# A fused attention and MLP block: layernorm's eps as a fifth triple of statistics, and another order of the first tiles' statistics and applies

## The chip, the core and the metric

The kernel runs on one core of a Trainium2 chip. A core has five engines that work side by side and tell each other by semaphores when something is done: TensorE (PE: matrix multiplications and transposes by a unit matrix; its weight loads are shown as PEld), VectorE (DVE), ScalarE (ACT), GpSimd (POOL) and SyncE (SP, which here only issues transfers). Each engine takes its instructions in the order in which the program lists them. The metric is the time of one execution on the device in microseconds (us), the median of several.

## The reference

```python
x = A_x                                   # 1 x 2048 x 640, bf16
xn = _layernorm(x, axis=-1)               # (x - mean) / sqrt(var + 1e-5)
return x + _A_ref(xn, A_wqkv, A_w_phi, A_wo) + _B_ref(xn, B_w1, B_w3, B_w2)

# _A_ref: linear attention, 32 heads of 20
q, k, v = ...                             # (xn @ wqkv), cut into heads
pq, pk = q @ w_phi, k @ w_phi             # per head, 20 x 20
phi_q = concatenate([softmax(pq), softmax(-pq)])
phi_k = concatenate([softmax(pk), softmax(-pk)])
kv, z = phi_k^T @ v, sum of phi_k over the tokens
o = (phi_q @ kv) / (phi_q @ z + 1e-6)
return o @ wo

# _B_ref: gated MLP, inner width 1536
return (silu(xn @ w1) * (xn @ w3)) @ w2
```

## The kernel before, in words

The 2048 tokens are cut into 16 tiles of 128, which lie on the 128 partitions. Each tile of x (x_tok) is normalized in place and then transposed into xnT, where the model dimension of 640 lies on the partitions in five chunks of 128. For the tiles 0 to 3 the transposes run on TensorE, with copies out of PSUM by ScalarE (three copies for tile 0, of two, two and one chunks; two copies for the others; one of tile 3's by VectorE); for the tiles 4 to 15 transfers do them.

From xnT come the values (wv), the keys (Wkp: the key weights with w_phi folded in), the queries (Wqp) and the MLP. Exponentials of the keys go to ekt and are divided by their sums (reduction on VectorE, multiplication on POOL). Then TensorE sums the products of keys and values over all tiles (tiles v,ekt in the profile), the queries are projected, normalized, transposed by a transfer (eqT) and multiplied with those sums. The MLP's matmuls of 128x512 (xnT,w_s) are spread between all this. At the end each output tile adds the attention's projection (wo), the MLP's second matmul (w2) and x itself (xres).

The order is made by a planner in the kernel. Fourteen streams (norms, transposes, attention, queries, mlps and others) offer their next step; `_Program` keeps a clock for each engine from the costs given with each operation, and the step that could begin first is taken. So a change in one early step can change the order of steps much later. What a step waits for is found from the memory that its operations read and write; the order on each engine is that in which the steps were taken. Almost all instructions are recorded by the two helpers `op` (line 102) and `dma` (line 114), so the profile shows them under L102 and L114, and one goes by the tiles' names.

What touches the start:

- `first_loads` issues tile 0 in two halves on SP, tile 1 on ScalarE's queue, then tile 2 on SP, the two halves of wv (one on each of the two queues), tile 3, and the first parts of w1 and w3 on SP.
- `warm_up` gives TensorE IDLE1 small matmuls on a tile of zeros (shown as `PS<-t`) before there is anything to do; after tile 0's transposes IDLE2 more follow.
- The statistics of a tile are two `bn_stats` of 320 columns each (`ln_half`; BATCH_NORM_STATS2 in the profile). Each leaves two triples in `bst`, for every second element: a count, a mean, and the count times the variance. `bn_aggr` (BATCH_NORM_AGGREGATE) merges the four triples into mean and variance (`mv`). Then eps is added, on VectorE for the tiles 0 to 3 and on POOL for the others, and POOL raises to the power -0.5 (`rstd`).
- Tile 1's statistics are ScalarE's: a sum (`act_sum` with Copy), which VectorE scales by -1/640 to the negative mean (`scalar_op`), and a sum of squares around that mean. `act_rstd` divides by 640, adds eps and takes the power.
- `ln_apply` subtracts the mean and multiplies by rstd: on VectorE for the tiles 0 to 3, on VectorE or ScalarE for the others, whichever the planner has free sooner.

The stream `norms` sets the order of the first steps:

```python
yield lambda: act_sum(1, ACT.Copy, bst[:, 1, 0:1])
yield lambda: (ln_half(0, 0), ln_half(0, 1), ln_rstd(0, 1))
yield lambda: scalar_op(1, mv[:, 1, 0:1], bst[:, 1, 0:1], -1.0 / D, 0.0)
yield lambda: act_sum(1, ACT.Square, mv[:, 1, 1:2], mv[:, 1, 0:1])
yield lambda: ln_apply(0)
yield lambda: act_rstd(1)
yield lambda: (ln_half(2, 0), ln_half(2, 1))
yield lambda: ln_apply(1)
```

Of the kernel before, what the change touches and what calls it, by code (L numbers as in the profile page):

```python
# [3 lines left out]
ACT = mybir.ActivationFunctionType  # L4
ALU = mybir.AluOpType
# [4 lines left out]
D = 640  # L10
# [3 lines left out]
T = S // 128  # L14
# [4 lines left out]
EPS = 1e-5  # L19
# [230 lines left out]
def bass_parallel_sum__linear_kernel_hedgehog__glu_gated_swiglu__prompt_kernel(  # L250
# [11 lines left out]
    bf = DT.bfloat16  # L262
    LAG = 4.0
    QLEAD = 2
    IDLE1, IDLE2 = 45, 5
    f32 = DT.float32
    P = _Program(nc)

# [5 lines left out]
    def region(size):  # L274
        o = top[0]
        top[0] = o + (size + 31) // 32 * 32
        assert top[0] <= arena_size, top[0]
        return a0 + o

    def new(name, shape, dtype, offset=None):  # L280
        size = mybir.dt.size(dtype)
        for n in shape[1:]:
            size *= n
        return P.sbuf(name, shape, dtype, region(size) if offset is None else offset)
# [2 lines left out]
    GM = new("GM", [128, DC, H], bf)  # L287
    phi_s = new("phi_s", [128, DC, DH], bf)
    BDc = new("BDc", [128, DC, 8 * DH], bf)
    bst = new("bst", [128, T, 12], f32)  # L290
    mv = new("mv", [128, T, 2], f32)
    rstd = new("rstd", [128, T, 2], f32)
    mhalf = new("mhalf", [128, 4], f32)
# [13 lines left out]
    x_tok = new("x_tok", [128, T, D], bf, RX)  # L307
# [53 lines left out]
    def free(ap):  # L361
        n = 1
        for s in ap.shape[1:]:
            n *= s
        return n

    def act(o, i, f, scale=1.0):
        P.op("ACT", "activation", [o], [i], (o, i, f), dict(scale=scale),
             cost=0.17 + free(o) / 1200)
# [21 lines left out]
    def memset(eng, o, v):  # L391
        P.op(eng, "memset", [o], [], (o, v), cost=0.15 + free(o) / 960)

    def select(o, base, pattern, cm, cmp, fill):
        P.op("POOL", "affine_select", [o], [o], (),
             dict(out=o, in_=o, compare_op=cmp, fill=fill, base=base, pattern=pattern,
                  channel_multiplier=cm), cost=0.3 + free(o) / 960)
# [16 lines left out]
    def first_loads():  # L414
        def half_wv(eng, a):
            P.dma(eng, wv[:, :, a:a + 320], wqkv_t[:, :, 2 * D + a:2 * D + a + 320])

        P.dma("SP", x_tok[:, 0, 0:320], x_t[:, 0, 0:320])
        P.dma("ACT", x_tok[:, 1, :], x_t[:, 1, :])
        P.dma("SP", x_tok[:, 0, 320:D], x_t[:, 0, 320:D])  # L420
        load_x(2, 3)
        half_wv("ACT", 0)
        half_wv("SP", 320)
        load_x(3, 4)
        w13(0, 512)
        P.dma("SP", phi_s[:], phi_t)
        P.dma("SP", wqkT[:, DC:2 * DC, :], A_wqkv[:, D:2 * D], True)
        load_x(4, 8)
        load_x(8, 12)
        load_x(12, 16)  # L430
        P.dma("SP", wqkT[:, 0:DC, :], A_wqkv[:, 0:D], True)


    def consts():
        memset("DVE", t1[:, 2, 0:128], 0.0)
        memset("DVE", warm[:], 0.0)
        act(warm[:], warm[:], ACT.Exp)
        memset("POOL", ident[:], 0.0)
        select(ident[:], 0, [[-1, 128]], 1, ALU.not_equal, 1.0)
        memset("POOL", GM[:], 1.0)  # L440
        select(GM[:], 0, [[128, DC], [-DH, H]], 1, ALU.is_ge, 0.0)
        select(GM[:], DH, [[-128, DC], [DH, H]], -1, ALU.is_gt, 0.0)
        memset("POOL", mhalf[:], -0.5)
        memset("POOL", M3[:, 0:3], 1.0)
        select(M3[:, 0:3], 0, [[-40, 3]], 1, ALU.is_ge, 0.0)
        select(M3[:, 0:3], 40, [[40, 3]], -1, ALU.is_gt, 0.0)
        memset("POOL", ekt[:, T * 2 * D:T * 2 * D + 48], 1.0)

    def v_heads(a):
        return a.rearrange("p (g x) -> p g x", x=64)[:, :, 0:63].rearrange("p g (h c) -> p g h c", c=21)  # L450

    def ln_half(t, q):
        i, o = x_tok[:, t, 320 * q:320 * q + 320], bst[:, t, 6 * q:6 * q + 6]
        P.op("DVE", "bn_stats", [o], [i], (o, i), cost=0.48)

    def ln_rstd(t0, n):
        for t in range(t0, t0 + n):
            o, i = mv[:, t, 0:2], bst[:, t, 0:12]
            P.op("DVE", "bn_aggr", [o], [i], (o, i), cost=0.22)
        m, v, r, z = mv[:, t0:t0 + n, 0], mv[:, t0:t0 + n, 1], rstd[:, t0:t0 + n, 0], rstd[:, t0:t0 + n, 1]  # L460
        if t0 < 4:
            P.op("DVE", "tensor_scalar", [r], [v], (),
                 dict(out=r, in0=v, scalar1=EPS, scalar2=None, op0=ALU.add), cost=0.13)
        else:
            P.op("POOL", "tensor_scalar_add", [r], [v], (r, v, EPS), cost=0.25)
        P.op("POOL", "tensor_tensor", [r], [r, mhalf[:, 0:n]], (r, r, mhalf[:, 0:n], ALU.pow),
             cost=0.57 if t0 < 4 else 0.73)
        if t0 >= 4:
            P.op("POOL", "tensor_scalar_mul", [z], [m], (z, m, -1.0), cost=0.25)
            P.op("POOL", "tensor_tensor", [z], [z, r], (z, z, r, ALU.mult), cost=0.25)  # L470

    def act_sum(t, f, o, bias=None):
        j = t1[:].rearrange("p n c -> p (n c)")[:, 0:D]
        i = x_tok[:, t, :]
        kw = dict(accum_out=o)
        if bias is not None:
            kw["bias"] = bias
        P.op("ACT", "activation", [j, o], [i] + ([] if bias is None else [bias]), (j, i, f), kw, cost=0.75)

    def scalar_op(t, o, i, a, b):  # L480
        P.op("DVE", "tensor_scalar", [o], [i], (),
             dict(out=o, in0=i, scalar1=a, scalar2=b, op0=ALU.mult, op1=ALU.add), cost=0.15)

    def act_rstd(t):
        scalar_op(t, rstd[:, t, 0:1], mv[:, t, 1:2], 1.0 / D, EPS)
        r = rstd[:, t, 0:1]
        P.op("POOL", "tensor_tensor", [r], [r, mhalf[:, 0:1]], (r, r, mhalf[:, 0:1], ALU.pow), cost=0.57)

    def ln_stats(t0, n):
        for t in range(t0, t0 + n):  # L490
            ln_half(t, 0)
            ln_half(t, 1)
        ln_rstd(t0, n)

    def ln_apply(t):
        o, m, s, z = x_tok[:, t, :], mv[:, t, 0:1], rstd[:, t, 0:1], rstd[:, t, 1:2]
        if t < 4 or P.free["DVE"] < P.free["ACT"] + 0.45:
            P.op("DVE", "tensor_scalar", [o], [o, m, s],
                 (o, o, m, s, ALU.add if t == 1 else ALU.subtract, ALU.mult),
                 cost=0.4)  # L500
        else:
            P.op("ACT", "activation", [o], [o, s, z], (o, o, ACT.Identity), dict(bias=z, scale=s),
                 cost=0.9)
# [227 lines left out]

    def norms():
        yield lambda: (first_loads(), consts())
        yield lambda: act_sum(1, ACT.Copy, bst[:, 1, 0:1])
        yield lambda: (ln_half(0, 0), ln_half(0, 1), ln_rstd(0, 1))
        yield lambda: scalar_op(1, mv[:, 1, 0:1], bst[:, 1, 0:1], -1.0 / D, 0.0)
        yield lambda: act_sum(1, ACT.Square, mv[:, 1, 1:2], mv[:, 1, 0:1])
        yield lambda: ln_apply(0)
        done["ln"] = 1
        yield lambda: act_rstd(1)  # L740
        yield lambda: (ln_half(2, 0), ln_half(2, 1))
        yield lambda: ln_apply(1)
        done["ln"] = 2
        yield lambda: ln_rstd(2, 1)
        yield lambda: ln_apply(2)
        done["ln"] = 3
        yield lambda: (ln_half(3, 0), ln_half(3, 1), ln_rstd(3, 1))
        yield lambda: ln_apply(3)
        done["ln"] = 4
        while done["t"] < 4:  # L750
            yield None
        yield lambda: memset("DVE", v_heads(v2[:].rearrange("p t n -> p (t n)"))[:, :, :, DH], 1.0)
        yield block_diag
        done["bd"] = 1
        todo = []
        for t in range(4, T + 2, 2):
            if t == T or t > done["k"] + 8:
                for u in todo:
                    yield lambda u=u: ln_apply(u)
                    done["ln"] = u + 1  # L760
                todo = []
            if t == T:
                break
            while t > done["k"] + 8:
                yield None
            yield lambda t=t: ln_stats(t, 2)
            for u in todo:
                yield lambda u=u: ln_apply(u)
                done["ln"] = u + 1
            todo = [t, t + 1]  # L770
# [166 lines left out]
    n = len(streams)  # L937
    heads, alive = [None] * n, [True] * n
    while any(alive):
        best = None  # L940
        for i in range(n):
            if heads[i] is None and alive[i]:
                s = next(streams[i], StopIteration)
# [28 lines left out]
        i, ops, after = best[2:]  # L972
# [65 lines left out]
```

## Time and profile before

| what | value |
|---|---|
| median of 3 runs | 268.09 us (268.03 to 268.10) |
| profiled execution | 267.97 us |
| its span, first to last instruction | 266.2 us |
| TensorE busy | 261.4 us, 98% of the span |
| VectorE, ScalarE, POOL busy | 168.0, 101.5, 100.6 us |
| granted TensorE clock | 1.000 over the span |
| HBM read, written | 12.81 MB, 2.62 MB |

How to read the lines that follow. A line of a group gives the engine, the operation, what it writes <- what it reads, partitions x elements, how often, the busy time in us and the mean of one in ns, and behind the second bar the idle time of the engine before it and what ended it. A line of the timeline gives start in us, duration in us, engine, line, operation, tiles; several instructions in a row are drawn together with their number behind an x, and the time from the first start to the last end. In brackets stands the idle time before. A line of the chain of waits gives start, duration and what it was. A line of the waits gives who waited for whom: us in total, how many times, the longest. A line on a transfer gives the queue, the size and the time from its issue to its landing. A line on one tile's instructions gives how many, their shortest, median and longest duration in ns, and the first and last start. Matmuls are pipelined: the duration of one is longer than the distance to the next. A few records of matmuls can be missing.

### The profile page before, as it was taken

The page shows a single profiled execution, that of the slowest core. Times are in us where ns is not written, and L with a number is a line of the kernel's source. Part 1 is how long each engine was busy: PE and PEld are TensorE (multiplying, and loading weights), DVE is VectorE, ACT ScalarE, POOL GpSimd, SP SyncE. Part 2 cuts the span into 40 slices and gives each one's busy share as a digit, 9 for nine tenths or more (in the row PEclk, how much of TensorE's full clock was granted, in tenths as well). Part 3 has the DMA queues.
Part 4 walks back from the last instruction along what each step waited for, and adds up shares of the span by engine and source line. Part 5 has one row for each costly group of instructions (what it writes and reads, how often), then busy time and mean ns, then how long its engine had stood idle before and what let it go on. Part 6 is the DMA issues. An engine that isn't in the chain of part 4 may idle for free.

```text
span 266.2 us, 4851 instructions
## 1 busy us (share of the span) xinstructions
PE 261.4 (98%) x1965; PEld 162.1 (61%) x1986; DVE 168.0 (63%) x289; ACT 101.5 (38%) x201; POOL 100.6 (38%) x143
## 2 busy tenths in 40 slices
PE   8999999999999999999999999999999999999996
PEld 7665777777655555545454545544577777777773
DVE  3469998998766979798898787888511121212112
ACT  5677999887326254433432343322100000000000
POOL 4314896999984444454624243430000000000000
PEclk9999999999999999999999999999999999999999
DMA  7998793760383254444454433063212212131201
GB/s 213 300 321 164 106 263 27 177 219 0 110 276 72 57 113 89 84 81 79 79 81 79 81 77 70 14 85 74 49 52 75 76 58 90 52 98 52 87 36 49
DMA packets 63510, 27.73 MB, mean 104 GB/s; under 512 B 49920, under 2 KB 63488, under 8 KB 63488
## 3 DMA queue, kind: packets, MB, share of 16 engines
q1 hardware_dynamic: 62544, 26.82, 43.6%
q10 hardware_dynamic: 944, 0.61, 0.7%
q8 instruction: 15, 0.25, 0.4%
q14 instruction: 7, 0.06, 0.1%
HBM read 12.81 MB, written 2.62 MB: 58 GB/s over the span
## 4 chain that ended last, share of the span: by engine, by line
PE 96%; DMA 1%; DVE 1%; issue 1%; POOL 0%
PE PS L102 96%; DMA x_tok<-in_A_x_dram 1%; DVE bst L102 0%; POOL rstd L102 0%; DVE x_tok L102 0%; DVE mv L102 0%; DVE xres L102 0%; DVE rstd L102 0%
## 5 line engine op out<-in xcount | busy, mean ns | idle before, releaser
L102 PE MATMUL PS<-xnT,w_s 128*128 128x512 bf16 x463 | 105.7, 379 | 1.0 <-issue 0.2
L102 PEld LDWEIGHTS PS<-xnT,w_s 128*128 128x128 bf16 x480 | 45.5, 98 | 50.7 <-DVE xnT L102 0.3
L102 PE MATMUL PS<-w_s,hT 128*128 128x320 bf16 (+2 forms) x384 | 54.9, 299 | 0.0
L102 DVE TENSOR_TENSOR xres<-PS,xres 128x640 bf16<-128x640 f32 (+2 forms) x17 | 13.4, 786 | 59.8 <-PE PS L102 59.8
L102 ACT ACTIVATE th<-PS 128x512 f32<-128x512 f32 x48 | 29.0, 603 | 49.8 <-PE PS L102 49.8
L102 PEld LDWEIGHTS PS<-w_s,hT 128*128 128x128 bf16 x384 | 37.1, 98 | 15.1
L102 DVE SCALAR_TENSOR_TENSOR t<-th,PS 128x512 bf16<-128x512 f32 x48 | 32.6, 680 | 16.0 <-ACT th L102 15.7
L102 POOL TENSOR_TENSOR ekt<-ekt,rS 128x640 bf16<-128x640 bf16 x32 | 39.6, 1276 | 2.6 <-DVE rS L102 2.6
L102 DVE SCALAR_TENSOR_TENSOR hT<-t,PS 128x512 bf16<-128x512 bf16 x48 | 33.0, 687 | 5.7 <-DVE t L102 0.9
L102 ACT ACTIVATE eq<-PS 128x600 bf16<-128x600 f32 (+1 forms) x72 | 23.9, 418 | 29.3 <-PE PS L102 29.3
L102 PE MATMUL PS<-wv,xnT 128*128 128x320 bf16 x160 | 24.5, 299 | 0.0
L102 PE MATMUL PS<-wo_s,oT 128*128 128x320 bf16 (+2 forms) x159 | 24.3, 298 | 0.1
L102 PE MATMUL PS<-Wqp,xnT 128*128 128x512 bf16 (+1 forms) x157 | 23.7, 297 | 0.2
L102 PE MATMUL PS<-Wkp,xnT 128*128 128x320 bf16 x160 | 23.7, 299 | 0.0
L102 POOL TENSOR_TENSOR eq<-eq,rq 128x600 bf16<-128x600 bf16 (+1 forms) x32 | 22.7, 730 | 1.3
L102 POOL TENSOR_TENSOR half<-eq 128x660 f32<-128x660 bf16 x15 | 20.4, 1359 | 7.0 <-ACT eq L102 7.0
L102 DVE TENSOR_REDUCE S<-ekt 128x64 f32<-128x1280 bf16 x16 | 22.9, 1432 | 0.0
L102 POOL TENSOR_TENSOR rq<-rq,Sq 128x32 f32<-128x32 f32 x16 | 4.1, 255 | 47.7 <-DVE rq L102 35.5
L102 ACT ACTIVATE ekt<-PS 128x640 bf16<-128x640 f32 x32 | 20.9, 733 | 2.5 <-PE PS L102 2.5
L102 PEld LDWEIGHTS PS<-Wqp,xnT 128*128 128x128 bf16 x160 | 13.2, 98 | 11.6
L102 PEld LDWEIGHTS PS<-wo_s,oT 128*128 128x128 bf16 x160 | 15.5, 98 | 6.5
L102 PEld LDWEIGHTS PS<-wv,xnT 128*128 128x128 bf16 x160 | 15.3, 98 | 6.3 <-ACT xnT L102 0.4
(56 smaller groups left out, 184.0 us busy)
## 6 DMA issues: line engine op xcount, KB each, us to landing
w_s<-in_B_w_dram SPq DMA_DIRECT2D x6, 640.0 KB, 6.1
xres<-in_A_x_dram SPq DMA_DIRECT2D x16, 160.0 KB, 2.4
out_dram<-xres SPq DMA_DIRECT2D x15, 160.0 KB, 1.8
x_tok<-in_A_x_dram SPq DMA_DIRECT2D x3, 640.0 KB, 6.4
w_s<-in_B_w_dram SPq DMA_DIRECT2D x1, 1920.0 KB, 8.4
wo_s<-in_A_wo_dram SPq DMA_DIRECT2D x1, 800.0 KB, 7.2
wv<-in_A_wqkv_dram ACTq DMA_DIRECT2D x1, 400.0 KB, 4.1
wv<-in_A_wqkv_dram SPq DMA_DIRECT2D x1, 400.0 KB, 5.2
```

The source lines that it names most:

```text
L102: o = _Op(eng, lambda: m(*args, **kw), r, w, cost)
```

## The change

Five edits.

1. `bst` gets three more columns per tile, a fifth triple: count 0, mean 0, and 640 x eps. `consts` writes them with two memsets on VectorE. `bn_aggr` reads 15 numbers instead of 12, so that its variance comes out with eps added. The additions of eps in `ln_rstd` (VectorE for the tiles 0, 2 and 3, POOL for 4 to 15) go, and POOL's power reads `mv` directly.
2. Tile 1's first sum on ScalarE gets the scale -1/640 and is written to `mv`; VectorE's scaling goes.
3. `ln_apply` takes a range of columns; tile 0 is applied in two parts, columns 0 to 255 and 256 to 639.
4. The first half of tile 2's statistics (`ln_half(2, 0)`) stands ahead of tile 0's apply; the second half stays where both were.
5. IDLE1 goes from 45 to 40 and IDLE2 from 5 to 2.

On VectorE the start reads then: four memsets, two `bn_stats` of tile 0, `bn_aggr` of tile 0, `bn_stats` of tile 2's first half, the two applies of tile 0, the division and eps of tile 1, `bn_stats` of tile 2's second half, apply of tile 1, `bn_aggr` and apply of tile 2. The transfers' issues at the start stay as they were. On TensorE the projections of the values between the transposes of the tiles 0, 1, 2 and 3 come in groups of 5, 7, 14 and 4 instead of 5, 8, 15 and 2. Later the planner puts some queries, MLP blocks and sums in another order, and ScalarE's applies of the tiles 4 to 7 stand in a row before the first exponentials of the keys, where two were before them and two behind; the matmuls are the same but for the small ones of edit 5.

```diff
-    IDLE1, IDLE2 = 45, 5
+    IDLE1, IDLE2 = 40, 2
...
-    bst = new("bst", [128, T, 12], f32)
+    bst = new("bst", [128, T, 15], f32)
...
         memset("DVE", warm[:], 0.0)
+        memset("DVE", bst[:, :, 12:14], 0.0)
+        memset("DVE", bst[:, :, 14:15], D * EPS)
...
-            o, i = mv[:, t, 0:2], bst[:, t, 0:12]
+            o, i = mv[:, t, 0:2], bst[:, t, 0:15]
...
-        if t0 < 4:
-            P.op("DVE", "tensor_scalar", [r], [v], (),
-                 dict(out=r, in0=v, scalar1=EPS, scalar2=None, op0=ALU.add), cost=0.13)
-        else:
-            P.op("POOL", "tensor_scalar_add", [r], [v], (r, v, EPS), cost=0.25)
-        P.op("POOL", "tensor_tensor", [r], [r, mhalf[:, 0:n]], (r, r, mhalf[:, 0:n], ALU.pow),
+        P.op("POOL", "tensor_tensor", [r], [v, mhalf[:, 0:n]], (r, v, mhalf[:, 0:n], ALU.pow),
...
-    def act_sum(t, f, o, bias=None):
+    def act_sum(t, f, o, bias=None, scale=1.0):
...
-        kw = dict(accum_out=o)
+        kw = dict(accum_out=o, scale=scale)
...
-    def ln_apply(t):
-        o, m, s, z = x_tok[:, t, :], mv[:, t, 0:1], rstd[:, t, 0:1], rstd[:, t, 1:2]
+    def ln_apply(t, a=0, b=D):
+        o, m, s, z = x_tok[:, t, a:b], mv[:, t, 0:1], rstd[:, t, 0:1], rstd[:, t, 1:2]
...
-                 cost=0.4)
+                 cost=0.06 + (b - a) / 1880)
...
-        yield lambda: act_sum(1, ACT.Copy, bst[:, 1, 0:1])
+        yield lambda: act_sum(1, ACT.Copy, mv[:, 1, 0:1], scale=-1.0 / D)
         yield lambda: (ln_half(0, 0), ln_half(0, 1), ln_rstd(0, 1))
-        yield lambda: scalar_op(1, mv[:, 1, 0:1], bst[:, 1, 0:1], -1.0 / D, 0.0)
         yield lambda: act_sum(1, ACT.Square, mv[:, 1, 1:2], mv[:, 1, 0:1])
-        yield lambda: ln_apply(0)
+        yield lambda: ln_half(2, 0)
+        yield lambda: (ln_apply(0, 0, 256), ln_apply(0, 256, D))
         done["ln"] = 1
         yield lambda: act_rstd(1)
-        yield lambda: (ln_half(2, 0), ln_half(2, 1))
+        yield lambda: ln_half(2, 1)
         yield lambda: ln_apply(1)
```

## The prediction

> **What bounds the kernel now.** I read the page first, then the chain of waits, then what TensorE (PE) waited for, then the start by its timeline and its transfers.
>
> The page: the span, TensorE's busy share, and two groups of the same multiplications, seen as matmuls and as weight loads.
>
> ```profile
> span 266.2 us, 4851 instructions
> PE 261.4 (98%) x1965; PEld 162.1 (61%) x1986; DVE 168.0 (63%) x289; ACT 101.5 (38%) x201; POOL 100.6 (38%) x143
> L102 PE MATMUL PS<-xnT,w_s 128*128 128x512 bf16 x463 | 105.7, 379 | 1.0 <-issue 0.2
> L102 PEld LDWEIGHTS PS<-xnT,w_s 128*128 128x128 bf16 x480 | 45.5, 98 | 50.7 <-DVE xnT L102 0.3
> ```
>
> TensorE is busy 98% of the span. Of 480 matmuls of this group 463 were recorded, so a hole of one matmul's length in a row of them can be a lost record. The waits of TensorE from 12 us to 264 us, all of them:
>
> ```profile
> PE PS L102 <- issue: 0.2, 1, 0.2
> ```
>
> So from 12 us to the end TensorE waits practically for nobody. Work taken from another engine there is worth nothing; the time can move only in the first 12 us, or if a new stall appears. The chain of waits shows what sets TensorE's start:
>
> ```profile
> 0.81 2.60 DMA x_tok<-in_A_x_dram
> ...
> 3.43 0.93 DVE bst L102 x2
> ...
> 4.38 0.22 DVE mv L102
> ...
> 4.63 0.15 DVE rstd L102
> ...
> 4.87 0.58 POOL rstd L102
> ...
> 5.48 0.45 DVE x_tok L102
> ...
> 6.00 0.72 PE PS L102 x10
> ...
> 6.74 5.09 PE PS L102 x45
> ```
>
> Tile 0 is loaded, summed up (DVE 3.43 to 4.36), aggregated, given eps, raised to -0.5 on POOL, applied (5.48 to 5.93), transposed (6.00) and projected (6.74). After that TensorE runs on. The profiled execution took 267.97 us, 1.77 more than its span; the median of the runs is 268.09, 0.12 above it.
>
> **The change part by part.** The rows of the start, from the timeline:
>
> ```profile
> 0.88 0.11 DVE L102 MEMSET t<- 128x64 uint32 x1 [0.88 <-PEq L1023]
> ...
> 4.29 0.19 ACT L102 ACTIVATION_READ_ACCUMULATOR t<-x_tok 128x1 f32 x1
> ...
> 4.88 0.83 ACT L102 ACTIVATE t<-x_tok,mv 128x640 bf16<-128x640 bf16 x1 [0.40 <-DVE mv L102]
> ...
> 5.90 0.88 DVE L102 BATCH_NORM_STATS2 bst<-x_tok 128x6 f32<-128x320 bf16 x2
> ...
> 6.06 0.56 POOL L102 TENSOR_TENSOR rstd<-rstd,mhalf 128x1 f32<-128x1 f32 x1 [0.62 <-DVE rstd L102]
> ...
> 6.30 0.83 ACT L102 ACTIVATE xnT<-PS 128x256 bf16<-128x256 bf16 x3 [0.51 <-PE PS L102]
> ...
> 6.70 0.43 DVE L102 TENSOR_SCALAR x_tok<-x_tok,mv,rstd 128x640 bf16<-128x640 bf16 x1
> 6.74 0.11 PEld L102 LDWEIGHTS PS<-wv,xnT 128*128 128x128 bf16 x2 [0.20 <-ACT xnT L102]
> 6.74 0.85 PE L102 MATMUL PS<-wv,xnT 128*128 128x320 bf16 x5
> ...
> 7.04 0.20 DVE L102 BATCH_NORM_AGGREGATE mv<-bst 128x2 f32<-128x12 f32 x1
> ...
> 7.43 0.44 PE L102 MATMUL PS<-ident,x_tok 128*128 128x128 bf16 x5
> 7.51 0.55 POOL L102 TENSOR_TENSOR rstd<-rstd,mhalf 128x1 f32<-128x1 f32 x1 [0.88 <-DVE rstd L102]
> ...
> 8.09 0.45 DVE L102 TENSOR_SCALAR x_tok<-x_tok,mv,rstd 128x640 bf16<-128x640 bf16 x1 [0.66 <-POOL rstd L102]
> ...
> 9.08 2.20 PE L102 MATMUL PS<-wv,xnT 128*128 128x320 bf16 x15
> ...
> 11.39 0.43 PE L102 MATMUL PS<-wv,xnT 128*128 128x320 bf16 x2
> 11.43 0.29 DVE L102 COPY xnT<-PS 128x256 bf16<-128x256 bf16 x1 [0.56 <-PE PS L102]
> ...
> 12.00 2.11 PE L102 MATMUL PS<-xnT,w_s 128*128 128x512 bf16 x9 [0.17 <-issue]
> ```
>
> *Eps as a fifth triple.* Two memsets more on DVE, about 0.11 us each; they lie before 3.43, where DVE waits for tile 0: cost nothing. In the first four tiles the addition of eps (0.15) and its hand-over go: tile 0's power follows the aggregate at 4.69 (its end at 4.60 and the 0.09 that lay between 4.78 and 4.87) instead of 4.87, and ends at 5.27. An aggregate over 15 numbers instead of 12 is not in the trace: 0.20 at the least, and, if all of it grew with the numbers, 0.26; I take 0.20, since the one-element operation of 0.15 shows that most of it is fixed. For tile 0 the 0.06 is covered by the wait below.
>
> *Tile 1's mean from ScalarE.* The scaling on DVE goes; ScalarE reads its own sum at 4.48 and squares from about 4.53 instead of 4.88, ending near 5.45. The scale rides in an instruction that runs anyway. Nothing is gained, since DVE takes that sum up only behind tile 0 (below).
>
> *Tile 2's statistics moved up.* The first half's BATCH_NORM_STATS2 now stands on DVE between tile 0's aggregate (end 4.60) and tile 0's apply, and it waits for tile 2's load. The transfers' issue and time to landing, tile 2's on SP and tile 1's of the same size on ScalarE's queue:
>
> ```profile
> 1.73 0.42 SPq L114 DMA_DIRECT2D x_tok<-in_A_x_dram  x1
> ```
>
> ```profile
> x_tok<-in_A_x_dram SPq DMA_DIRECT2D x1, 160.0 KB, 3.9
> ```
>
> ```profile
> x_tok<-in_A_x_dram ACTq DMA_DIRECT2D x1, 160.0 KB, 2.8
> ```
>
> Issued at 1.73 and 3.9 us under way, tile 2 lands at 5.65. Before, its statistics ran at 5.90 and never waited. No transfer's issue is moved on SP or ScalarE in this stretch, so I keep 5.65. Then DVE stands from 4.60 to 5.65 with tile 0's apply queued behind, though POOL has rstd at 5.27. The statistics start at 5.67 and hold DVE 0.40 (the pair of 5.90 took 0.88, and the next instruction came 0.80 after its start): apply begins at 6.07 instead of 5.48, 0.59 late. Everything that the first item gained is lost in this wait.
>
> *Tile 0's apply in two parts.* 256 columns lie between one element (0.15) and 640 (0.45): by a straight line 0.27. First part 6.07 to 6.34, where the whole ended at 5.93: TensorE's first transpose, and the first copy and projection behind it, come 0.41 late. Bounds: with 0.15 it is 0.29, with 0.45 0.59. The second part of 384 columns (0.33) starts near 6.25 and ends at 6.58; the third transpose follows at 6.64 and the second copy could begin at 6.90, but ScalarE is in the first until 6.99 (copies follow each other by 0.28). So the second part costs nothing.
>
> *What follows.* The first projection starts at 7.15 (6.74 + 0.41), and its five end such that tile 1's transposes get their turn at 7.84. Tile 1: eps on DVE behind the second part at 6.49 to 6.64, power at 6.72 to 7.28, apply 7.31 to 7.76, ready at 7.82: not late. The second half of tile 2's statistics fits into that power's time. Tile 2: aggregate at 7.66 (7.04 came 0.35 after apply began), power 7.94 to 8.49 without the addition of eps, apply 8.53 to 8.98, ready at 9.03; TensorE gets there, with seven projections instead of eight between, at 9.08. Margin 0.05, which the unknown 0.06 of the aggregate could just use up. Tile 3 by the same steps is ready about 11.2, TensorE there at 11.26.
>
> *The refilled hole.* Before, the two projections of 11.39, 0.136 apart (from 15 in 2.20), end their turn at 11.67; of the ten matmuls that follow nine are recorded, so the first stood at 12.00 - 0.216 = 11.79, after the copy of 11.43 to 11.72. Hole: 0.12. Now four projections stand there (one each fewer in the two groups before), TensorE is through them at 12.08, and that copy is done at 11.86. The hole goes: 0.12 back.
>
> *Fewer filling matmuls* (40 for 45, 2 for 5): they fill waiting, worth nothing by themselves; see the clock below.
>
> *The order later on.* The same matmuls in another order. One check: the last four key tiles are summed after 30 matmuls of 128x512 instead of 40, so at 78.11 - 2.16 + 0.29 = 76.24, its last tile 0.96 later.
>
> ```profile
> 69.52 6.19 POOL L102 TENSOR_TENSOR ekt<-ekt,rS 128x640 bf16<-128x640 bf16 x5
> ```
>
> ```profile
> 78.11 1.43 PE L102 MATMUL PS<-v,ekt 128*128 128x63 bf16 x44
> ```
>
> POOL has the last key tile at 75.71, needed at 77.20: 1.5 us of room, so nothing, if POOL is not over 1.5 later.
>
> *Sum.* +0.59 (apply later) - 0.18 (first part shorter and sooner) - 0.12 (hole) = +0.29: 268.26 against the profiled 267.97, and 268.38 against the median, say 268.4. With the bounds of the first part 268.26 to 268.56. A difference of 0.2% (0.54 us) is about what a measurement of this kernel can tell from no change, so this case counts as within it.
>
> **The rivals.**
>
> *The load is there in time, and the start gets faster.* If tile 2 takes the 2.8 us of tile 1's load of the same size, it lands at 4.53, before DVE is free at 4.60. Then apply starts at 5.30, its first part ends at 5.57 (5.93 before), and all following steps move by -0.36, with the hole -0.48: 267.6. It holds in full for a landing below about 4.9, where the statistics end before rstd comes; a landing at 5.36 would leave the time as it was (5.65 less the 0.29 of the sum). Against it: 3.9 is measured here, and no transfer is moved.
> [...]
>
> *The clock opens late, and it is slower.* The filling matmuls' own durations, early and late:
>
> ```profile
> L102 PE MATMUL PS<-t x40: 289/314/314, 1.1 to 5.2; 128*128 128x128 bf16 x40
> ```
>
> ```profile
> L102 PE MATMUL PS<-t x11: 219/219/314, 5.2 to 6.5; 128*128 128x128 bf16 x11
> ```
>
> They take 314 ns until about 5.4 and 219 after: TensorE becomes fast some 4.35 us after its first matmul, while matmuls still run. The new 40 end at 1.05 + 40 x 0.107 = 5.32, just short of it, and TensorE then idles until 6.40. If the opening has to be earned anew from 6.40, it comes at 10.75, and 3.6 us of work from 7.15 on runs at half rate: +1.8, 270.2. It decides if the activity up to 5.32 isn't enough. For it: only 0.1 us is missing. Against it: 4.3 us of work are nearly all, and the runs before agree within 0.07.
> [...]
>
> *A stall in the rearranged middle.* ScalarE now applies tiles 4 to 7 in a row, ahead of the first key tile's exponentials.
>
> ```profile
> 22.97 1.72 ACT L102 ACTIVATE x_tok<-x_tok,rstd 128x640 bf16<-128x640 bf16 x2
> ```
>
> Two applies more are 1.72: the exponentials, and POOL's chain behind them, start up to 1.7 + 0.3 later, 2.0, against the room of 1.5: 0.5 of stall, 268.9. It decides if POOL can't make up 0.5 us on the way; three additions of eps that leave POOL behind that point make it likely that it can.
>
> *The load lands still later:* each tenth adds a tenth; above 5.9 it is slower by over 0.2%.
>
> **How the numbers follow.** Start late by 0.2 to 0.5, nothing else: 0.58 (268.26 to 268.56, its own range). Load in time: 0.10 (at 267.6, half of it counted as faster). Clock late: 0.13. Stall in the middle: 0.13. Load later: 0.06. Faster 0.05, same 0.63, slower 0.32. The range from 268.0 to 269.4 leaves out the load in time and the larger part of the late clock, 0.2 together.
>
> **What will show it.** On DVE, the statistics ahead of tile 0's apply waiting for x_tok's load until 5.65, the first part of apply at 6.07, transposes at 6.40, the first projection at 7.15; no hole near 12; the first 128x512 matmul 0.29 later than before; no waits of TensorE after 12. The prediction is wrong if DVE doesn't wait there, if projections behind 7.15 are 0.27 apart instead of 0.136, or if TensorE shows new waits between 60 and 190.

## The result, and the profile after

The changed kernel takes 269.37 us in the median of 22 executions, the kernel before 268.12 in as many: ratio 1.0046, 95% interval 1.003 to 1.0062, slower. The median is a time that no execution has. The executions of the changed kernel fall into two groups, eleven from 268.29 to 268.80 and eleven from 269.93 to 270.65; those of the kernel before lie from 267.91 to 268.43. The profiled execution of the changed kernel took 270.03, so it is one of the second group. Four of that group (270.23, 270.31, 270.58 and 270.65) have a mean granted clock of 0.994; all other executions of this kernel, the profiled one too, have 1.000. What the 0.994 stands for shows in the last experiment.

The page of the changed kernel:

```profile
span 268.3 us, 4826 instructions
PE 263.0 (98%) x1958; PEld 162.7 (61%) x1978; DVE 166.8 (62%) x287; ACT 101.5 (38%) x202; POOL 99.0 (37%) x137
```

TensorE is still busy 98%, and its busy time grew by 1.6 us although it has eight small matmuls less to do: some of them took longer. The chain of waits shows what sets the start now:

```profile
1.73 3.76 DMA x_tok<-in_A_x_dram
...
5.51 0.49 DVE bst L102
6.00 0.26 DVE x_tok L102
...
6.31 7.49 PE PS L102 x52
```

Where tile 0's load, statistics, aggregate, eps, power and apply stood, there is now tile 2's load, issued at 1.73, and the statistics that wait for it. The start by the timeline (in brackets the idle time before, and what ended it):

```profile
4.47 0.22 DVE L102 BATCH_NORM_AGGREGATE mv<-bst 128x2 f32<-128x15 f32 x1
...
4.78 0.57 POOL L102 TENSOR_TENSOR rstd<-mv,mhalf 128x1 f32<-128x1 f32 x1 [1.53 <-DVE mv L102]
...
5.51 0.49 DVE L102 BATCH_NORM_STATS2 bst<-x_tok 128x6 f32<-128x320 bf16 x1 [0.81 <-DMA x_tok<-in_A_x_dram]
5.92 0.62 DVE L102 TENSOR_SCALAR x_tok<-x_tok,mv,rstd 128x256 bf16<-128x256 bf16 x2
...
6.31 0.79 PE L102 MATMUL PS<-ident,x_tok 128*128 128x128 bf16 x5 [0.81 <-DVE x_tok L102]
...
7.18 1.51 PE L102 MATMUL PS<-wv,xnT 128*128 128x320 bf16 x5
```

POOL has rstd at 5.35, and apply begins at 5.92. The first projection comes at 7.18, 0.44 later than before. The five projections there take 1.51 us where they took 0.85. How long the matmuls of the start are, before and after 10.4 us, by groups:

```profile
L102 PE MATMUL PS<-wv,xnT 128*128 128x320 bf16 x10 | 3.0, 466 | 0.0
```

```profile
L102 PE MATMUL PS<-wv,xnT 128*128 128x320 bf16 x21 | 3.5, 306 | 0.0
```

The first row is from 7.1 to 10.3 us, the second from 10.4 to 13.7: 466 ns for one, then 306. The filling matmuls of this execution, as one tile's instructions (shortest, median and longest duration, first and last start):

```profile
L102 PE MATMUL PS<-t x42: 287/314/314, 1.1 to 7.0; 128*128 128x128 bf16 x42
```

All 42 last some 314 ns, to the last at 7.0. The first matmul of full rate starts at 10.35. The profile's granted clock doesn't show this: it reads 1.00 from 7.0 to 10.3 us too, so the rate has to be read from the matmuls' durations and distances. Ten projections 0.267 apart instead of 0.136 and five transposes 0.107 apart instead of 0.056 cost 1.56 us. Further on there is one new gap:

```profile
46.94 0.48 PE L102 MATMUL PS<-BDc,wqkT 128*128 128x140 bf16 x6
47.45 1.26 PE L102 MATMUL PS<-Wkp,xnT 128*128 128x320 bf16 x8
```

```profile
44.25 2.54 ACT L102 ACTIVATE x_tok<-x_tok,rstd 128x640 bf16<-128x640 bf16 x3
46.68 0.71 ACT L102 ACTIVATE v<-PS 128x660 bf16<-128x660 f32 x1
```

The key projection follows the folding of the query weights 0.51 after its start. In the kernel before it was 0.31:

```profile
45.09 0.48 PE L102 MATMUL PS<-BDc,wqkT 128*128 128x140 bf16 x6
45.40 1.52 PE L102 MATMUL PS<-Wkp,xnT 128*128 128x320 bf16 x10
```

ScalarE does three applies in a row here (two before), so the values' copy out of PSUM comes late, and TensorE waits 0.2, for room there. That it waits for this copy is inferred, for the list of waits has no row for it: the copy ends at 47.39 and the projection starts at 47.45, and in three other kernels below whose profiles have this gap (the statistics back with 40 filling matmuls, fifty, and eps alone) the projection also starts 0.05 to 0.06 behind the end of that copy. The sum closes: 0.44 (start) - 0.12 (the hole near 12 us) + 1.56 (clock) + 0.2 (gap) = 2.08, against 270.03 - 267.97 = 2.06 measured.

### The profile page after: what moved, and what is told of

Its sections match the earlier page's. It is cut to its first block, busy times and chain, and to the rows that moved or that the text cites. A ratio compares the mean times of both kernels' runs of the same rounds, so it can differ in the third digit from the quotient of the medians.

```text
span 268.3 us, 4826 instructions
## 1 busy us (share of the span) xinstructions
PE 263.0 (98%) x1958; PEld 162.7 (61%) x1978; DVE 166.8 (62%) x287; ACT 101.5 (38%) x202; POOL 99.0 (37%) x137
## 4 chain that ended last, share of the span: by engine, by line
PE 96%; DMA 1%; issue 1%; DVE 0%; SPq 0%
PE PS L102 96%; DMA x_tok<-in_A_x_dram 1%; SPq L114 0%; DVE bst L102 0%; DVE xres L102 0%; DVE x_tok L102 0%
## 5 line engine op out<-in xcount | busy, mean ns | idle before, releaser
L102 PE MATMUL PS<-wv,xnT 128*128 128x320 bf16 x160 | 25.8, 309 | 0.0
L102 PEld LDWEIGHTS PS<-wv,xnT 128*128 128x128 bf16 x160 | 15.9, 101 | 6.8 <-ACT xnT L102 0.2
L102 PEld LDWEIGHTS PS<-Wkp,xnT 128*128 128x128 bf16 x160 | 15.4, 98 | 6.1 <-ACT v L102 0.2
```

The source lines that it names most:

```text
L102: o = _Op(eng, lambda: m(*args, **kw), r, w, cost)
```

## The experiments

"Late" stands here for an execution that lies over 0.5 us above the rest of the same kernel. "Theory (gap)" in the expectations is my assumption that TensorE's pause ahead of the transposes, 0.81 us in the profile of the changed kernel, makes the full rate come late in a part of the executions.

**Fifty filling matmuls instead of forty.** The order of all else is kept.

```diff
-        for i in range(n):
+        for i in range(n + (10 if n == IDLE1 else 0)):
```

> The changed kernel with 50 filling matmuls ahead of tile 0's transposes instead of 40, everything else in the same order. [...] Then 50 (to 5.9 when the clock opens at 5.4, to 6.4 when it doesn't) close the pause: one cluster, 268.3 to 268.9, and none near 270. Rival (middle): the slow executions come from the rearranged order later on; then clusters at 268.4 and 270.2 stay as they are.

Eleven executions from 268.44 to 269.01, median 268.57, ratio to the kernel before 1.0017 (1.0008 to 1.0026). No execution near 270. This profiled execution, too, got its full rate late, at 7.0, but before the first projection:

```profile
6.89 0.35 PE L102 MATMUL PS<-t 128*128 128x128 bf16 x2
7.25 0.86 PE L102 MATMUL PS<-wv,xnT 128*128 128x320 bf16 x5
```

The five projections take 0.86 again. So the second group comes from the pause of TensorE ahead of the transposes, and not from the order later on, which is the same here.

**Forty filling matmuls in the kernel before.**

```diff
-    IDLE1, IDLE2 = 45, 5
+    IDLE1, IDLE2 = 40, 2
```

> The kernel before with 40 and 2 filling matmuls instead of 45 and 5, nothing else. Theory (gap): the pause ahead of the transposes is 0.5 to 0.7 us, between that of before (0.2) and that of the changed kernel (0.8 to 1.1): fast executions as before at 268.1, and a fifth to two fifths slow, near 269.5. Rival (count): half of them slow. Rival (middle): no slow ones, 268.1 throughout.

Eight of eleven at 267.93 to 268.34, as before; 268.85, 269.98 and 272.13 for the other three; median 268.07, ratio 1.0009 (0.9994 to 1.0023). How much of this is the edit is not clear from these eleven: 268.85 is no more than the slowest of the 33 executions of the kernel before that were taken beside them (268.86), and 272.13 is farther off than any late opening seen here explains, and there is no trace of it. That leaves 269.98; the next experiment is the clear one. The profiled execution of this kernel, at 268.03, shows something else, the filling matmuls from 3.6 to 5.4 us:

```profile
L102 PE MATMUL PS<-t x18: 219/219/314, 3.4 to 4.5; 128*128 128x128 bf16 x18
```

Here the clock opened at 3.69 (the first filling matmul of 219 ns), 2.6 us after the first matmul, not at 5.4: the moment belongs to the execution, not to the kernel.

**Thirty.**

```diff
-    IDLE1, IDLE2 = 45, 5
+    IDLE1, IDLE2 = 30, 2
```

> The kernel before with 30 and 2 filling matmuls: they end near 4.3, 3.2 us after the first, and TensorE pauses for 1.7 us. [...] Rival (work adds up, pauses don't matter): the 30 count, and a part of the executions stays at 268.1 to 268.5. The filling itself is worth its time only by the clock.

Four of twelve at 267.90 to 268.02, eight from 269.08 to 270.60, median 269.09, ratio 1.0036 (1.0018 to 1.0053). More late ones than with 40, as the theory has it, and none such among the 29 of the kernel before beside them (267.86 to 268.44): the edit which I had costed at nothing does make executions late. But I had expected every execution to be late, from 269.3 to 271.3, and four are not. That rested on a length of work without a pause which I took the full rate to need, and no run shows one. In the profiled execution, at 267.98, the transposes behind the pause are quick already:

```profile
L102 PE MATMUL PS<-ident,x_tok x5: 219/219/231, 5.9 to 6.2; 128*128 128x128 bf16 x5
```

The 30 filling matmuls, from 1.05 to 4.43, all ran at half rate, so here the full rate opened at their end or during the pause of 1.5 us, and the rest of that pause did no harm in this execution. It isn't always so: two of the late ones, both of 269.67, have a mean granted clock of 0.994 (see the last experiment).

**Tile 2's statistics back behind tile 0's apply**, with 40 filling matmuls.

```diff
-        yield lambda: ln_half(2, 0)
         yield lambda: (ln_apply(0, 0, 256), ln_apply(0, 256, D))
...
-        yield lambda: ln_half(2, 1)
+        yield lambda: (ln_half(2, 0), ln_half(2, 1))
```

> The changed kernel with the first half of tile 2's statistics behind tile 0's apply again; 40 filling matmuls stay. Theory (wait for tile 2's load): tile 0's apply starts near 5.35 instead of 5.92, the transposes near 5.7, and the fast executions take 267.6 to 267.8. Theory (gap): the pause shrinks to 0.2 to 0.4 us, and at most a quarter of the executions are slow. Rival (count): 40 filling matmuls (4.3 us) are too few whatever follows; then half of the executions are slow, by about 1.5, as in the changed kernel. Rival (load hidden): fast executions stay at 268.4.

Nine of eleven from 267.87 to 268.04, two at 268.63 and 268.83; median 267.94, ratio 0.9998 (0.9989 to 1.0007). VectorE in this kernel's timeline:

```profile
4.30 0.22 DVE L102 BATCH_NORM_AGGREGATE mv<-bst 128x2 f32<-128x15 f32 x1
5.22 0.64 DVE L102 TENSOR_SCALAR x_tok<-x_tok,mv,rstd 128x256 bf16<-128x256 bf16 x2 [0.69 <-POOL rstd L102]
```

Apply begins at 5.22 instead of 5.92 and waits only for POOL. Late ones are rarer and milder than the 11 of 22, with the same 40: it is not their count, it is what follows them. (Two such are hardly more than the kernel before has: 268.61 and 268.86 among its 33.) But the nine are 0.2 above the 267.6 to 267.8 that I expected; the gap of 0.2 in the middle is in this kernel too (next but one).

**The same with 44 and 5 filling matmuls.**

```diff
-        for i in range(n):
+        for i in range(n + (4 if n == IDLE1 else 3)):
```

> The changed kernel with tile 2's first half behind tile 0's apply again and 44 and 5 filling matmuls, the order of all else kept. Theory (gap): the last filling matmul ends near 5.75, the transposes begin near 5.65 to 5.75, no pause: one cluster at 267.85 to 268.1 and none above 268.5. Rival (chance): the two runs of 268.6 and 268.8 with 40 had another cause, and one or two such runs are seen again.

Eleven from 267.87 to 268.15, median 267.93, ratio 0.9995 (0.9986 to 1.0003). One group, as expected.

**And one apply given back to VectorE.**

```diff
-        if t < 4 or P.free["DVE"] < P.free["ACT"] + 0.45:
+        if t < 4 or P.free["DVE"] < P.free["ACT"] + 0.60:
```

> As the one before, and the planner's margin for giving an apply to ScalarE from 0.45 to 0.6, which moves one apply of a later tile from ScalarE back to VectorE, so that ScalarE has two in a row near 43 us instead of three. Theory (stall in the middle): the 0.2 us that TensorE loses near 45 us behind the folding of the query weights goes: 267.65 to 267.85, 0.2 under the one before. Rival: the gap there is a lost record or has another cause; no difference.

Eleven from 267.65 to 268.17, median 267.72; ratio to the kernel before (268.04 beside it) 0.9989, 0.9981 to 0.9998. TensorE near 45 us in this kernel:

```profile
44.84 0.48 PE L102 MATMUL PS<-BDc,wqkT 128*128 128x140 bf16 x6
45.15 1.11 PE L102 MATMUL PS<-Wkp,xnT 128*128 128x320 bf16 x7
```

0.31 again instead of 0.51, and 0.21 less in the median: the gap was real. This is the fastest version found, 0.3 us or 0.1% under the kernel before.

**Eps as the fifth triple alone, in the kernel before.**

```diff
-            o, i = mv[:, t, 0:2], bst[:, t, 0:12]
+            o, i = mv[:, t, 0:2], bst[:, t, 0:15]
...
-        if t0 < 4:
-            P.op("DVE", "tensor_scalar", [r], [v], (),
...
```

> The kernel before with eps as the fifth triple alone (45 and 5 filling matmuls, apply in one part, statistics of tile 2 behind it). Theory: the start gains 0.2 (no addition of eps) and the 0.1 of the hole near 12; the planner, which sees POOL free sooner, puts three applies of later tiles on ScalarE in a row near 43 us, and TensorE loses 0.2 there: 267.85 to 268.05, one cluster, with a gap of 0.2 between the folding of query weights and the next key projection near 45. Rival: the stall in the middle belongs to another edit; then no gap there, 267.65 to 267.85.

Twelve from 267.96 to 268.14, median 268.04 (268.11 before beside it), ratio 0.9995 (0.9986 to 1.0003): no difference that can be told, and the gap is there:

```profile
44.86 0.48 PE L102 MATMUL PS<-BDc,wqkT 128*128 128x140 bf16 x6
45.37 0.85 PE L102 MATMUL PS<-Wkp,xnT 128*128 128x320 bf16 x5
```

So it is this edit which moves an apply to ScalarE; that the planner does so because it sees other engines free sooner is likely, but not shown. The gap takes 0.2 (0.51 against 0.31) and the median is 0.07 lower, so by estimate the edit gains 0.27 elsewhere, which the expectation puts at the start, and gives 0.2 back at 45 us.

**Only the move of tile 2's statistics, in the kernel before.**

```diff
+        yield lambda: ln_half(2, 0)
         yield lambda: ln_apply(0)
...
-        yield lambda: (ln_half(2, 0), ln_half(2, 1))
+        yield lambda: ln_half(2, 1)
```

> The kernel before with the first half of tile 2's statistics ahead of tile 0's apply, nothing else (45 and 5 filling matmuls). Theory (wait for tile 2's load): apply starts near 6.0 instead of 5.48, the first projection 0.45 to 0.55 late, 0.1 of it given back in the hole near 12: fast executions at 268.4 to 268.6. Theory (gap): the pause grows from 0.2 to 0.6 to 0.7, so some executions are slow, near 270. Rival (load hidden): 268.1, no slow ones.

Seven of eleven from 268.25 to 268.41, three at 268.80 to 268.87, one at 271.09; median 268.41, ratio 1.002 (1.0002 to 1.0039). The move alone makes the kernel slower, by 0.3 in most executions. The one of 271.09 has a granted clock of 0.994, the same as in the last experiment, so its rate probably fell back behind the longer pause; no trace of it was taken, and for the three at 268.8 no trace says why. VectorE in the profiled execution, at 268.41:

```profile
5.54 0.49 DVE L102 BATCH_NORM_STATS2 bst<-x_tok 128x6 f32<-128x320 bf16 x1 [0.71 <-DMA x_tok<-in_A_x_dram]
5.95 0.43 DVE L102 TENSOR_SCALAR x_tok<-x_tok,mv,rstd 128x640 bf16<-128x640 bf16 x1
```

**The wait alone:** the changed kernel with 50 filling matmuls and the planner's margin of 0.60, so with neither the late clock nor the gap near 45.

> The changed kernel with 50 filling matmuls and the planner's margin of 0.6, so that neither the clock nor the stall near 45 takes part, and only the wait for tile 2's load is left. Theory (wait for tile 2's load): 0.5 to 0.65 above the kernel that has the statistics back and the same margin (267.72): 268.25 to 268.4 for most executions. Rival: the wait is covered by the rest of the start; 267.7 to 267.9.

Twelve from 268.15 to 269.06, median 268.38, ratio 1.0011 (1.0003 to 1.0019). Against 267.72 of the kernel that differs from it in the place of tile 2's statistics and in the number of filling matmuls, 0.66; with each held against the kernel before beside it (268.11 and 268.04), 0.59. It was expected at 0.5 to 0.65.

**Tile 2's load earlier**, on ScalarE's queue ahead of half of wv, with 44 and 5 filling matmuls and the changed kernel's order of statistics.

```diff
-        load_x(2, 3)
+        P.dma("ACT", x_tok[:, 2, :], x_t[:, 2, :])
         half_wv("ACT", 0)
```

> The changed kernel with its own order of statistics, tile 2's load issued on ScalarE's queue behind tile 1's and ahead of wv's half, and 44 and 5 filling matmuls. Theory (wait for tile 2's load): it lands near 4.7 to 5.0, VectorE waits 0.1 to 0.4 at the most instead of 0.8 to 1.0, apply starts near 5.3 to 5.45: 267.7 to 268.0, one cluster. Rival (load not the cause): apply still starts near 5.9, 268.4.

Four executions from 271.88 to 272.55, median 272.15, ratio 1.0151 (1.0138 to 1.0164). The cause of the wait was right and the forecast wrong. VectorE, and then TensorE, in this kernel's timeline:

```profile
4.51 0.43 DVE L102 BATCH_NORM_STATS2 bst<-x_tok 128x6 f32<-128x320 bf16 x1
5.28 0.64 DVE L102 TENSOR_SCALAR x_tok<-x_tok,mv,rstd 128x256 bf16<-128x256 bf16 x2 [0.34 <-POOL rstd L102]
```

```profile
9.57 0.84 PE L102 MATMUL PS<-wv,xnT 128*128 128x320 bf16 x5 [2.57 <-DMA wv<-in_A_wqkv_dram]
```

```profile
wv<-in_A_wqkv_dram ACTq DMA_DIRECT2D x1, 400.0 KB, 7.7
```

Statistics and apply no longer wait for the load; but wv's half, issued by estimate 0.4 us later than before (tile 1's issue of 160 KB held ScalarE's queue from 0.81 to 1.24 there), needs 7.7 us to land instead of the 4.1 of the kernel before, and the first projection waits for it until 9.57. The transfers behind on SP's queue were issued sooner by the same edit, by estimate 0.5 us (tile 2's issue held that queue from 1.73 to 2.19), and the run doesn't separate the two. After that pause the matmuls from 10.3 on ran at half rate again, and this time the granted clock shows it (stretch, its length, busy time of TensorE with its matmuls, granted clock, share of the DMA engines, GB/s):

```profile
10.30:13.60 3.30, 3.30 (x20) 0.50 1.25 223
```

The five projections before had run at full rate (from 9.57, in 0.84), so here the rate fell back after it had opened. These 3.3 us at 0.50 in a span of 270.8 make a mean of 0.994, and this is the mean of all four executions of this kernel. By the same sum, the four executions of the changed kernel with 0.994 are probably ones whose rate had opened early and fell back behind the pause; of these no trace was taken.

## Why the prediction was right or wrong

The forecast was 268.4, with a range of 268.0 to 269.4, and a difference within 0.2% as the likeliest. The measured 269.37 lies at the range's upper end, and the kernel is slower by 0.46%. So the likeliest case describes half of the executions and was not the outcome. That the median lies inside the range at all is luck: with eleven executions in each group it is the middle between 268.80 and 269.93, and one late execution more among the 22 would have put it above 269.9.

*Tile 2's statistics moved up: right.* VectorE waits for tile 2's load, rstd lies ready meanwhile, and what the removal of eps gains is lost there. The load landed at 5.49 (1.73 + 3.76) instead of 5.65, the statistics held VectorE 0.41, apply began at 5.92, 0.15 sooner than forecast.

*Apply in two parts: mis-sized.* By a straight line the first part was to take 0.27; it took 0.33, and the whole 0.45 before. By groups:

```profile
L102 DVE TENSOR_SCALAR x_tok<-x_tok,mv,rstd 128x256 bf16<-128x256 bf16 x1 | 0.3, 330 | 0.0
```

So splitting gains 0.12 there, not 0.18. That the first projection came out at 7.18 against the forecast 7.15 is a coincidence: apply began sooner, but the transposes ran at half rate in this execution. In the kernel before, whose transposes ran at full rate, it came 0.76 behind the first transpose (5.98 to 6.74), here 0.87 (6.31 to 7.18): at full rate it would by estimate have come at 7.07.

*Eps: right at the start* (the power at 4.78, 0.08 behind the aggregate, which took 223 ns with 15 numbers, 209 with 12), *wrong in that the order later on costs nothing.* I had named a stall in the rearranged middle as a rival of 0.5 at the key sums, with 0.13. It is there, but near 45 us and of 0.2, through the applies that the planner gave to ScalarE; in the key sums there is none. What failed here is that I had checked one place of the new order, and not the room of the copies near the applies that moved.

*The sum: right for the executions in which the clock opens in time.* With the gap and the clock taken out, the wait and the rest make 268.38 against 268.11 measured beside it, +0.27 (0.08 to 0.51 by the interval of the ratio); the forecast was +0.29. The agreement is closer than its terms, of which apply came 0.15 sooner and splitting gained 0.06 less. With the gap of 0.2 the fifty-filler kernel has +0.44. The changed kernel's own first group lies from 268.29 to 268.80; forecast 268.26 to 268.56.

*Fewer filling matmuls "worth nothing by themselves": wrong, and this is the step because of which the likeliest case failed.* The rival "the clock opens late" was there, with 270.2 as its time; its group lies from 269.93 to 270.65, with 270.2 in the middle. I gave it 0.13, and the group is half of the executions. The range up to 269.4 counts a smaller part of this rival as lying inside it; no run shows a time for such a part, and in the changed kernel the late executions begin at 269.93, all of them above the range. Seven of these eleven have a granted clock of 1.000 like the profiled one, in which the rate opened late as this rival has it; the four with 0.994 are probably a second kind, a rate that had opened and fell back, which the prediction doesn't name. Both come with the pause: in the 23 executions with 50 filling matmuls neither was seen.

Two things led to the low chance. I took the moment of the opening, 5.4, from the one profile as a property of the kernel, and reasoned that 5.32 is almost enough. The profiles show openings at 3.69 (40 in the kernel before), 5.40 (the kernel before), 7.00 (fifty) and 10.35 (the changed kernel), and by estimate at 4.1 with the statistics back, where the 40 filling matmuls ended at 4.92; all begin at 1.05. And I read the agreement of three runs within 0.07 as evidence that the opening is steady; it more likely meant that the kernel before, with a pause of 0.2 in its profile, rarely suffers wherever the opening falls (1 late of 107).

Late ones by the pause between the end of the filling matmuls, taken at 107 ns each up to the end of the last (314 ns long), and the transposes: hardly any where they would reach the transposes (1 of 107 of the kernel before in all rounds, at 269.02; none of 57 in the five other kernels), 2 of 11 at 0.1 in the statistics-back kernel with 40, 1 of 11 at 0.4 (the move alone, with three more at 0.4 us above the rest), 3 of 11 at 0.5 (40 in the kernel before; two of them doubtful, see there), 11 of 22 at 0.8 (the changed kernel), 8 of 12 at 1.5 (30 in the kernel before). These are the pauses at half rate; where the rate opens early the filling ends sooner and the pause is longer, 1.29 us in the profile that opened at 3.69.

What decides when the full rate opens was not shown. In the changed kernel it came at 10.35, 4.0 us behind the end of the pause of 0.81; with 40 in the kernel before at 3.69, 2.6 us behind the first matmul; and with 30 the transposes ran at full rate right behind a pause of 1.5 us. So neither a fixed moment nor a fixed length of work since the last pause fits the runs.

*The load is there in time: excluded as forecast*, since no transfer's issue moved. The kernel that did move it shows both that the statistics then wait for nothing (they start at 4.51, the aggregate ahead of them at 4.37) and that a transfer behind pays for it (7.7 us to landing instead of 4.1). Tile 2's load took 3.76 to 3.9 us in the changed kernel and the one before.

## What to carry to other kernels

A profile is one execution: a moment that differs from execution to execution (here when TensorE's full rate opens, 3.7 to 10.4 us) must be taken as a range, and late executions were rare here (1 of 164) only where the filling work reached without a pause from the first matmul to the real work, also if it ran at half rate all the way; with a pause of 0.8 us they were 11 of 22. An instruction that is moved up on an in-order engine has to be held against the landing of its data, not against the free time of its engine: 0.8 us of waiting came from 0.4 us of moved work. Where a planner orders the work, an edit that only removes operations may still cost something elsewhere, and the whole new order near the moved operations has to be compared.

## What the runs showed that was not expected

- A two-peaked time on a single core: 268.29 to 268.80 and 269.93 to 270.65, from one pause of 0.8 us or more in the first 7 us.
- The full rate fell back behind a pause of 2.57 us (granted clock 0.50 from 10.3 to 13.6, in the kernel with tile 2's load earlier). The granted clock showed this fall, but not the half rate ahead of the first opening (1.00 from 7.0 to 10.3 us in the changed kernel).
- The full rate opened 2.6 us after the first matmul in one execution (3.69 against 1.05, 40 in the kernel before).
- With one 160 KB load ahead of it on its queue, taken off the other queue, a 400 KB load needed 7.7 us to landing instead of 4.1 in the kernel before; the kernel took 4 us longer, some of it by the half rate behind the wait.
- VectorE's apply (TENSOR_SCALAR, bf16) takes 330 ns for 256 columns, 375 ns for 384 and 430 to 446 ns for 640: by estimate 0.3 ns a column above some 250 ns.
